# Attention feeding a channel-mix MLP: score banks held as three PSUM tiles of two banks, the last query tile of two head pairs as one group, the value product in the MLP's two banks

## The chip, the cores and the metric

The kernel runs on one core of one Trainium2 chip. The metric is device time in microseconds (us) of one execution. The engines that matter are TensorE (PE; its weight loads are listed as PEld), VectorE (DVE), ScalarE (ACT), GpSimd (POOL) and SyncE (SP, which here only issues DMAs). PSUM, where TensorE writes, has eight banks of 512 float32 per partition; a bank is what one matrix product is summed in. Each engine takes its instructions in the order in which they stand in its own queue.

## The reference, cut to what matters

All arrays are float32. Batch 8, 12 heads, sequence 448, head size 64; the MLP (called "MoE" in the code) has width 768 and inner width 1024.

```python
q_n, k_n = rmsnorm(q, g_q), rmsnorm(k, g_k)
scores = q_n @ k_n.T / sqrt(64)
attn = softmax(scores)
x = (attn @ v) laid out as [8, 448, 768]      # heads side by side
x_prev = x shifted by one position, zero first
xk = mu_k * x + (1 - mu_k) * x_prev
xr = mu_r * x + (1 - mu_r) * x_prev
out = sigmoid(xr @ w_r) * (relu(xk @ w_k) ** 2 @ w_v)
```

## The kernel before, in words

**Precision.** Every operand of a large product is split into a high and a low float16 half, and each product is three matmuls (high by high, high by low, low by high), summed in PSUM.

**Units of work.** Attention goes by head *pairs* (six per batch, 48 in all); two pairs form a *quad*, which shares the load and the normalisation of q and k (`prep`, L162 to L194: ACT squares, POOL and DVE sums, a reciprocal square root on DVE whose small operands lie in a PSUM bank called `misc`, and DMA transposes into the tiles `stk`). The 448 queries of a pair are seven tiles of 64. A *group* is two such tiles for both heads, 128 rows of scores per bank: `group_scores` (L240) issues six matmuls into two PSUM banks named `sc`, then for each bank a maximum on DVE (L260) and the exponential with its row sum on ACT (L261). The seventh tile of a pair is a group by itself, with one bank. `group_probs` (L265) takes the reciprocal of the sums (L273, L274), writes the high half of the probabilities on ACT (L279) and the low half on DVE (L280) into `ph`, and one DMA transpose (two for the seventh tile, L286) puts them into `pT`. After a pair's last group `attend` (L291) makes the value product, 22 matmuls into a bank named `av`, and ACT copies it out (L305).

**Scale of v.** `vprep` (L196) finds a power of two for each pair's v: a square with row sum on ACT, one small matmul into the `av` bank (L207), a maximum from there on DVE (L209), three small DVE operations, then the halves `vh` and `vl`.

**The MLP.** `moe(b)` (L450) runs behind attention. Its products are tiles named `mm`, in a ring of two banks: eight tiles of 18 matmuls for xk by w_k, then tiles of 18 (xr by w_r) and 24 (kk by w_v), all from line L460; ACT (L482, L516) or DVE (L519) reads a tile out. In the first part of the run the weights are converted as well (`weight_tile`, L394): they use the `mm` ring and, for their scales, the `av` bank.

**PSUM.** One bank `misc`, one `av`, four `sc`, two `mm`.

**What sets the order.** Three generators (attention, weights, MLP) are stepped in turn by a clock of their own: an attention step counts 1/126 of a batch (`ATT_STEPS`), an MLP step 1/93, and the MLP of batch b starts at b + 1.25. That gives the program order. A scheduler then places the instructions of each engine by its own timing model; those of the scores are preferred by 400 places (`QK_PRIORITY`). What program order fixes in any case is who gets a bank next: tiles of one name take the buffers of their ring in turn, so the third `mm` tile can start only when the first has been read out.

## Time and profile before

| | |
|---|---|
| median of three runs | 1214.28 us (1214.15 to 1221.72) |
| profiled execution, own time | 1216.88 us |
| its span, first to last instruction | 1215.1 us |
| mean granted TensorE clock | 0.934 |
| first value product read out | 91.0 us |
| 14th of 48 | 399.5 us |
| 48th of 48 | 1128.0 us |
| from there to the end (the MLP alone) | 87.1 us |

The run has three stretches. Up to some 300 us the weights are converted beside attention. From then to 1128 us attention and the MLP share TensorE. Then the MLP of the last batch runs alone. A row of the views by group reads: line, engine, operation, output tile from input tiles, shapes, count, then busy time and mean of one, then the idle time of the engine just before these instructions and what ended it.

### The profile page before, as it was taken

The page shows a single profiled execution, that of the slowest core. Times are in us where ns is not written, and L with a number is a line of the kernel's source. Part 1 is how long each engine was busy: PE and PEld are TensorE (multiplying, and loading weights), DVE is VectorE, ACT ScalarE, POOL GpSimd, SP SyncE. Part 2 cuts the span into 40 slices and gives each one's busy share as a digit, 9 for nine tenths or more (in the row PEclk, how much of TensorE's full clock was granted, in tenths as well). Part 3 has the DMA queues.
Part 4 walks back from the last instruction along what each step waited for, and adds up shares of the span by engine and source line. Part 5 has one row for each costly group of instructions (what it writes and reads, how often), then busy time and mean ns, then how long its engine had stood idle before and what let it go on. Part 6 is the DMA issues. An engine that isn't in the chain of part 4 may idle for free. (4 is left out here: it accounts for less than half of the span.)

```text
span 1215.1 us, 18885 instructions
## 1 busy us (share of the span) xinstructions
PE 996.6 (82%) x5935; PEld 476.4 (39%) x5935; DVE 828.9 (68%) x2357; ACT 794.8 (65%) x1756; POOL 672.3 (55%) x678
## 2 busy tenths in 40 slices
PE   1135545686788899999999999999899799999998
PEld 0012222243344344443444444444444354445464
DVE  4577788887977577676877676857775578666200
ACT  3366668677767767677778776777687477865411
POOL 2644357645558645585657564765586257523821
PEclk9996566888989999999999999999999899999999
DMA  7898889978789878878988897797897887885001
GB/s 160 147 182 169 162 165 218 191 152 151 143 139 161 152 123 162 150 129 158 162 154 154 155 170 141 134 167 146 143 157 129 128 148 135 137 158 90 13 14 39
DMA packets 456356, 172.77 MB, mean 142 GB/s; under 512 B 411200, under 2 KB 452672, under 8 KB 456256
## 3 DMA queue, kind: packets, MB, share of 16 engines
q1 hardware_dynamic: 423328, 132.24, 64.2%
q10 hardware_dynamic: 32928, 39.34, 13.8%
q8 instruction: 46, 0.75, 0.3%
q14 instruction: 54, 0.44, 0.1%
HBM read 61.41 MB, written 11.01 MB: 60 GB/s over the span
## 5 line engine op out<-in xcount | busy, mean ns | idle before, releaser
L261 ACT ACTIVATE sc<-sc,sums 128x448 f32<-128x448 f32 x336 | 201.6, 608 | 108.0 <-DVE sums L260 99.4
L280 DVE SCALAR_TENSOR_TENSOR ph<-sc,sums,ph 128x448 f16<-128x448 f32 x336 | 218.3, 677 | 68.4 <-ACT ph L279 66.1
L238 PE MATMUL sc<-stk 64*128 64x448 f16 (+1 forms) x1152 | 190.3, 380 | 68.3 <-DVE ph L280 45.9
L460 PE MATMUL mm<-wvh,kk 128*128 128x384 f16 x896 | 236.5, 332 | 4.0 <-DVE th L519 4.0
L460 PE MATMUL mm<-xk,wkh 128*128 128x448 f16 x768 | 217.8, 363 | 11.6 <-ACT kf L482 10.1
L260 DVE TENSOR_REDUCE sums<-sc 128x1 f32<-128x448 f32 x336 | 196.3, 613 | 37.3 <-PE sc L238 36.7
L279 ACT ACTIVATE ph<-sc,sums 128x448 f16<-128x448 f32 x336 | 195.2, 642 | 31.9 <-DMA pT<-ph 10.1
L238 PE MATMUL av<-pT,vh 128*64 128x448 f16 x672 | 145.8, 387 | 63.4 <-DMA pT<-ph 49.9
L460 PE MATMUL mm<-wrh,xr 128*128 128x384 f16 x672 | 177.1, 327 | 3.1 <-ACT xr L377 2.4
L460 PEld LDWEIGHTS <-kk 128*128 128x128 f16 x1344 | 126.5, 99 | 111.2 <-issue 36.6
L460 PE MATMUL mm<-wvl,kk 128*128 128x384 f16 x448 | 148.9, 332 | 0.0
L460 PE MATMUL mm<-xk,wkl 128*128 128x448 f16 x384 | 139.2, 363 | 0.0
L189 POOL TENSOR_TENSOR nat<-qk,nat 128x896 f16<-128x896 f32 x48 | 91.3, 1903 | 67.6 <-ACT nat L187 67.6
L238 PEld LDWEIGHTS <-stk 64*128 64x128 f16 (+1 forms) x1152 | 56.0, 100 | 184.1 <-issue 138.9
L170 POOL TENSOR_TENSOR xs<-xs 128x448 f32<-128x448 f32 x48 | 55.7, 1160 | 127.1 <-ACT xs L169 126.8
L460 PEld LDWEIGHTS <-xr 128*128 128x128 f16 x1008 | 93.6, 98 | 78.8 <-issue 16.2
L375 DVE SCALAR_TENSOR_TENSOR df<-x,bsc,df 128x448 f32<-128x448 f32 x90 | 90.3, 1014 | 32.7 <-POOL df L374 32.1
L273 DVE TENSOR_SCALAR sums<-sc 128x1 f32<-128x1 f32 x336 | 49.6, 151 | 89.9 <-ACT sc L261 88.5
L182 POOL TENSOR_TENSOR qk<-qk,ss 128x896 f32<-128x896 f32 x48 | 80.1, 1689 | 54.8 <-DVE ss L70 44.7
L460 PE MATMUL mm<-wrl,xr 128*128 128x384 f16 x336 | 109.7, 327 | 0.0
L460 PEld LDWEIGHTS <-wkh 128*128 128x128 f16 x768 | 73.9, 100 | 91.3 <-issue 35.5
L238 PEld LDWEIGHTS <-vh 128*64 128x64 f16 x672 | 59.5, 117 | 113.7 <-issue 67.3
(117 smaller groups left out, 1576.8 us busy)
## 6 DMA issues: line engine op xcount, KB each, us to landing
vf<-in_v_dram SPq DMA_DIRECT2D x48, 224.0 KB, 3.8
qk<-in_k_dram ACTq DMA_DIRECT2D x48, 224.0 KB, 4.8
qk<-in_q_dram ACTq DMA_DIRECT2D x48, 224.0 KB, 5.1
out_dram<-o SPq DMA_DIRECT2D x56, 192.0 KB, 2.9
vf<-in_v_dram SPq DMA_DIRECT2D x48, 192.0 KB, 3.8
raw<-in_moe_w_k_dram ACTq DMA_DIRECT2D x16, 384.0 KB, 4.4
raw<-in_moe_w_v_dram ACTq DMA_DIRECT2D x12, 512.0 KB, 4.4
raw<-in_moe_w_r_dram ACTq DMA_DIRECT2D x12, 384.0 KB, 4.7
```

The source lines that it names most:

```text
L170: nc.gpsimd.tensor_tensor(out=xs[:, :, 0:HD // 2], in0=xs[:, :, 0:HD // 2], in1=xs[:, :, HD // 2:], op=ALU.add)
L182: nc.gpsimd.tensor_tensor(out=tv, in0=tv, in1=spread(y[:, 2 * NT * n:2 * NT * (n + 1)], HD), op=ALU.mult)
L189: nc.gpsimd.tensor_tensor(out=lo, in0=t4, in1=hi, op=ALU.subtract)
L238: return op(**kw)
L260: nc.vector.tensor_reduce(out=sums[:, t:t + 1], in_=sp[:, 0:S], axis=AX.X, op=ALU.max, negate=True)
L261: nc.scalar.activation(out=sp[:, 0:S], in_=sp[:, 0:S], func=AF.Exp, bias=sums[:, t:t + 1], accum_out=sp[:, S:S + 1])
L273: nc.vector.tensor_scalar(out=r[:, j:j + 1], in0=sp[:, S:S + 1], scalar1=1e-9, scalar2=2.0 ** -15, op0=ALU.add, op1=ALU.mult)
L279: nc.scalar.activation(out=ph[:, j, 0:S], in_=sp[:, 0:S], func=AF.Copy, scale=r[:, j:j + 1])
L280: nc.vector.scalar_tensor_tensor(out=ph[:, j, S:], in0=sp[:, 0:S], scalar=r[:, j:j + 1], in1=ph[:, j, 0:S], op0=ALU.mult, op1=ALU.subtract)
L375: nc.vector.scalar_tensor_tensor(out=df, in0=xc, scalar=sc[:, MX + j:MX + j + 1], in1=df, op0=ALU.mult, op1=ALU.add)
L460: nc.tensor.matmul(out=ps_, lhsT=la(i, a), rhs=ra(i, c), start=(i == 0 and a + c == 0), stop=(i == n - 1 and a == 1))
```

## The change

The `misc` and `av` banks go. Two banks remain for the ring `mm`, and six go to scores, as three tiles of two banks.

- **Scores.** A group always fills one two-bank tile. `scores` takes one maximum over both banks in one DVE instruction, and `probs` one operation for both row sums. There are two exponentials and two copies per group as before.
- **Seventh tile.** The seventh query tiles of the two pairs of a quad form one group of twelve matmuls, placed fourth of seven groups. Four small transposes follow it, as two followed each of the two groups before. A quad has seven groups in place of eight.
- **Value product, scale of v, weight scales.** They take their bank from the ring `mm`, in turn with the MLP's tiles and the weights'. The small matmul for the scale of the next pair's v is written into the last 64 columns of the value product's bank, right behind the product, and ACT copies it to SBUF (a new instruction for each pair), where DVE takes the maximum. The square for it is issued at the end of the pair before, and `vprep` of a pair runs during that pair's own first groups. The load of the next pair's v is issued inside `vprep`.
- **prep.** The small operands of the reciprocal square root lie in SBUF.
- **Counts.** `ATT_STEPS` is 123; attention has 117 steps per batch, where it had 120 and `ATT_STEPS` was 126. The six xk tiles of a batch's last pair are mixed three and three, not in three twos.

The diff, cut to its core:

```diff
-ATT_STEPS = 126
+ATT_STEPS = 123
...
-    misc = ps.tile([P, 512], F32, name="misc", bufs=1)
-
     def allmax(src, n, r):
-        pt = ps.tile([P, 512], F32, name="av", bufs=1)
+        pt = ps.tile([P, 512], F32, name="mm", bufs=MM_BUFS)
...
-    rsqrt(nc, gm[:, 1:2], misc[:, 510:511], misc[:, 511:512])
+    rsqrt(nc, gm[:, 1:2], gm[:, 0:1], gm[:, 5:6])
...
-        o = (u % 2) * 2 * NSS
-        ss, tm = misc[:, o:o + NSS], misc[:, o + NSS:o + 2 * NSS]
+        sst = small.tile([P, 2 * NSS], F32, name="sst", bufs=2)
+        ss, tm = sst[:, 0:NSS], sst[:, NSS:]
...
+    def vsquare(i):
+        vf = VF[i]
+        vh = ap_.tile([P, 2, NT, HD], F16, name="vh", bufs=2)
+        vs = small.tile([P, 2 + HD], F32, name="vs", bufs=2)
+        nc.scalar.activation(out=vh[0:HD].rearrange("p h t d -> p h (t d)").bitcast(BF16), in_=vf[0:HD], func=AF.Square, accum_out=vs[0:HD, 0:1])
+        VS[i] = vh, vs
+
+    def vsum(i, dst):
+        vs = VS[i][1]
+        nc.tensor.matmul(out=dst, lhsT=vs[0:HD, 0:1].bitcast(BF16)[:, 1:2].broadcast_to([HD, P]), rhs=ident16[0:HD, 0:HD], start=True, stop=True)
+        nc.scalar.copy(out=vs[:, 2:], in_=dst)
...
         if hp == 0:
             BS[b] = small.tile([P, 2 * NP], F32, name="bstat", bufs=3)
         st = BS[b]
         vf = VF.pop(i)
-        vh = ap_.tile([P, 2, NT, HD], F16, name="vh", bufs=2)
+        vh, vs = VS.pop(i)
         vl = ap_.tile([P, 2, 4, HD], F16, name="vl", bufs=2)
-        vs = small.tile([P, 2], F32, name="vs", bufs=2)
-        pt = ps.tile([P, 512], F32, name="av", bufs=1)
-        nc.scalar.activation(out=vh[0:HD].rearrange("p h t d -> p h (t d)").bitcast(BF16), in_=vf[0:HD], func=AF.Square, accum_out=vs[0:HD, 0:1])
-        nc.tensor.matmul(out=pt[:, 0:HD], lhsT=vs[0:HD, 0:1].bitcast(BF16)[:, 1:2].broadcast_to([HD, P]), rhs=ident16[0:HD, 0:HD], start=True, stop=True)
-        yield
-        nc.vector.tensor_reduce(out=vs[:, 1:2], in_=pt[:, 0:HD], axis=AX.X, op=ALU.max)
         sv, iv = st[:, hp:hp + 1], st[:, NP + hp:NP + hp + 1]
+        nc.vector.tensor_reduce(out=vs[:, 1:2], in_=vs[:, 2:], axis=AX.X, op=ALU.max)
...
+        if i + 1 < len(pairs):
+            vload(i + 1)
         yield
...
-    def group_scores(i, t0, n):
-        T = TQ[i]
-        if t0 == 0:
-            SUMS[i] = small.tile([P, 32], F32, name="sums")
-        sums = SUMS[i]
-        banks = []
-        for j in range(n):
-            banks.append(ps.tile([P, 512], F32, name="sc", bufs=4))
+    def scores(g):
+        u, x, t0 = g
+        both = ps.tile([P, 2, 512], F32, name="sc", bufs=3)
+        sums = small.tile([P, 4], F32, name="sums", bufs=6)
...
             for m, (kl, ql) in enumerate(((0, 0), (0, 1), (1, 0))):
-                for h in (1, 0):
-                    hs = slice(h * HD, (h + 1) * HD)
-                    last = after(last, nc.tensor.matmul,
-                        out=banks[h][:, 0:S] if n == 2 else banks[0][hs, 0:S],
-                        lhsT=T[hs, 1, ql * NT + t0:ql * NT + t0 + n].rearrange("p t c -> p (t c)"),
-                        rhs=T[hs, 0, kl * NT:(kl + 1) * NT].rearrange("p t c -> p (t c)"),
-                        start=(m == 0), stop=(m == 2))
-        for j, sp in enumerate(banks):
-            t = t0 + j
-            nc.vector.tensor_reduce(out=sums[:, t:t + 1], in_=sp[:, 0:S], axis=AX.X, op=ALU.max, negate=True)
-            nc.scalar.activation(out=sp[:, 0:S], in_=sp[:, 0:S], func=AF.Exp, bias=sums[:, t:t + 1], accum_out=sp[:, S:S + 1])
-            SC[i, t] = sp
-            yield
-
-    def group_probs(i, t0, n):
-        sums = SUMS[i]
-        if t0 == 0:
-            PT[i] = ap_.tile([P, 2, NT, S], F16, name="pT", bufs=PT_BUFS)
-        pT = PT[i]
-        r = sums[:, 16 + t0:16 + t0 + n]
-        sps = [SC.pop((i, t0 + j)) for j in range(n)]
-        for j, sp in enumerate(sps):
-            nc.vector.tensor_scalar(out=r[:, j:j + 1], in0=sp[:, S:S + 1], scalar1=1e-9, scalar2=2.0 ** -15, op0=ALU.add, op1=ALU.mult)
+                for i in (2 * u + x,) if t0 < NT - 1 else (2 * u, 2 * u + 1):
+                    T = TQ[i]
+                    for h in range(2):
+                        hs = slice(h * HD, (h + 1) * HD)
+                        if t0 < NT - 1:
+                            dst, n = both[:, h, 0:S], 2
+                        else:
+                            o = (h + i % 2) % 2 * HD
+                            dst, n = both[o:o + HD, i % 2, 0:S], 1
+                        last = after(last, nc.tensor.matmul, out=dst,
+                            lhsT=T[hs, 1, ql * NT + t0:ql * NT + t0 + n].rearrange("p t c -> p (t c)"),
+                            rhs=T[hs, 0, kl * NT:(kl + 1) * NT].rearrange("p t c -> p (t c)"),
+                            start=(m == 0), stop=(m == 2))
+        nc.vector.tensor_reduce(out=sums[:, 0:2], in_=both[:, :, 0:S], axis=AX.X, op=ALU.max, negate=True)
+        SC[g] = both, sums
+        for j in range(2):
+            nc.scalar.activation(out=both[:, j, 0:S], in_=both[:, j, 0:S], func=AF.Exp, bias=sums[:, j:j + 1], accum_out=both[:, j, S:S + 1])
+            yield
+
+    def probs(g, gi):
...
+        for i in (2 * u + x,) if t0 < NT - 1 else (2 * u, 2 * u + 1):
+            if i not in PT:
+                PT[i] = ap_.tile([P, 2, NT, S], F16, name="pT", bufs=PT_BUFS)
+        r = sums[:, 2:4]
+        nc.vector.tensor_scalar(out=r, in0=both[:, :, S], scalar1=1e-9, scalar2=2.0 ** -15, op0=ALU.add, op1=ALU.mult)
...
-        for j in range(n):
-            sp = sps[j]
...
+        for j in range(2):
+            nc.scalar.activation(out=ph[:, j, 0:S], in_=both[:, j, 0:S], func=AF.Copy, scale=r[:, j:j + 1])
+            nc.vector.scalar_tensor_tensor(out=ph[:, j, S:], in0=both[:, j, 0:S], scalar=r[:, j:j + 1], in1=ph[:, j, 0:S], op0=ALU.mult, op1=ALU.subtract)
+        if t0 < NT - 1:
             nc.sync.dma_start_transpose(
-                out=pT.rearrange("p a c r -> p (a c) r")[:, :, t0 * HD:(t0 + n) * HD], in_=ph.rearrange("p a c -> p (a c)"))
+                out=PT[2 * u + x].rearrange("p a c r -> p (a c) r")[:, :, t0 * HD:(t0 + 2) * HD], in_=ph.rearrange("p a c -> p (a c)"))
...
+            for y in range(2):
+                for h in range(2):
+                    o = (h + y) % 2 * HD
+                    nc.sync.dma_start_transpose(out=PT[2 * u + y][:, h, :, t0 * HD:], in_=ph[o:o + HD, y, :])
+        yield
...
-        av = ps.tile([P, 512], F32, name="av", bufs=1)
+        av = ps.tile([P, 512], F32, name="mm", bufs=MM_BUFS)
...
+        if i + 1 < len(pairs):
+            with tc.issue_after(last.ins):
+                vsum(i + 1, av[:, S:])
...
+        NQ = len(quads)
+        groups = [(u, *g) for u in range(NQ) for g in ((0, 0), (0, 2), (0, 4), (0, NT - 1), (1, 0), (1, 2), (1, 4))]
...
+        vsquare(0)
+        av = ps.tile([P, 512], F32, name="mm", bufs=MM_BUFS)
+        vsum(0, av[:, S:])
+        yield
         yield from vprep(0)
...
+        pre = vp = iter(())
+        yield from scores(groups[0])
+        for gi, g in enumerate(groups):
+            u, x, t0 = g
+            i = 2 * u + x
+            if x == 0 and t0 == 0 and u + 1 < NQ:
+                pre = prep(u + 1)
+            if gi and t0 == 0:
+                vp = vprep(i)
...
+            next(vp, None)
+            yield
+            done = (t0 == NT - 1) if x == 0 else (t0 == NT - 3)
+            if done:
+                for h in (vp,) + ((pre,) if x else ()):
+                    for _ in h:
                         yield
-                if i + 2 < N:
-                    vload(i + 2)
+                if i + 1 < len(pairs):
+                    vsquare(i + 1)
                 if x and u + 2 < NQ:
                     load(u + 2)
             if gi + 1 < len(groups):
-                yield from group_scores(*groups[gi + 1])
-            yield from group_probs(i, t0, n)
-            if t0 == 6:
+                yield from scores(groups[gi + 1])
+            yield from probs(g, gi)
+            if done:
                 yield from attend(i)
             b, hp = pairs[i]
-            if hp == NP - 1 and t0 >= 2:
...
-        for d in {2: (0, 1), 4: (2, 3), 6: (4, 5)}[t0]:
+        for d in {2: (0, 1, 2), 4: (3, 4, 5)}[t0]:
...
-        pg = ps.tile([P, 512], F32, name="av", bufs=1)
+        pg = ps.tile([P, 512], F32, name="mm", bufs=MM_BUFS)
```

What this does to the order on TensorE is seen at two places. The rows give line, operation, output tile from its inputs with buffer numbers, and the output's size; `xr` and `kk` are the MLP's inputs, `wr` and `wv` its weights, `pT` the transposed probabilities, `vh` and `vl` the halves of v, `stk` the transposed q and k.

First, before the change, at the value product of the 29th pair:

```order
L460 MATMUL mm_7670<-wrh_109,xr_5206 128x384
L460 LDWEIGHTS xr_5206
L460 MATMUL mm_7670<-wrl_110,xr_5206 128x384
L238 LDWEIGHTS vh_6843
L238 MATMUL av_7233<-pT_7045,vh_6843 64x448
L460 LDWEIGHTS xr_5206
L460 MATMUL mm_7670<-wrh_109,xr_5206 128x384
L460 LDWEIGHTS xr_5206
L460 MATMUL mm_7670<-wrh_109,xr_5206 128x384
```

One matmul of the value product stands alone between matmuls of the MLP; seven MLP matmuls follow it, then the other 21. The changed kernel, at the value product of the same pair:

```order
L244 MATMUL mm_6983<-pT_6804,vh_6688 64x448
L244 LDWEIGHTS vl_6776
L244 MATMUL mm_6983<-pT_6804,vl_6776 64x448
L244 LDWEIGHTS stk_6928
L244 MATMUL sc_7192<-stk_6928 128x448
L244 LDWEIGHTS stk_6928
L244 MATMUL sc_7192<-stk_6928 128x448
```

Here the value product is cut by scores, which come in whole groups of six, and no MLP matmul stands inside it. Over the whole program the sequence of large and small matmuls changes its kind (scores, value product, MLP, weights, scale of v) 684 times before and 423 times now: 685 and 424 stretches. Up to the 14th value product it is 155 and 127 of them. Up to the 14th value product the MLP has had 444 of its 3504 matmuls before and 414 now; up to the 48th and last 3034 and 2718, so that 470 and 786 are left behind it. Between a pair's last score and its value product stand, over pairs 15 to 48, 58.5 MLP matmuls in the median (41 at least) before, and 115.5 (67 at least) now.

Second, the ring of two banks, in the changed kernel, at the end of the value product of the 30th pair:

```order
L244 MATMUL mm_7223<-pT_6966,vh_6946 64x448
L202 LDWEIGHTS vs_7184
L202 MATMUL mm_7223<-ident16_75,vs_7184 128x64
L474 LDWEIGHTS kk_5095
L474 MATMUL mm_7176<-wvh_109,kk_5095 128x384
...
L474 MATMUL mm_7176<-wvh_109,kk_5095 128x384
L474 LDWEIGHTS xr_5020
L474 MATMUL mm_7273<-wrh_107,xr_5020 128x384
```

Behind the value product in tile 7223 come the scale of v and the last six matmuls of tile 7176, and then at once the first matmul of tile 7273, which has the bank of 7176: it must wait until DVE has read 7176 out. Among the 38 places where a value product stands between two MLP tiles in the ring, 9 have no matmul at all between the earlier tile's last matmul and the next use of its bank. Before the change no tile of the MLP follows so closely.

43 lines of the change are left out of this document (12 added, 31 removed).

## The prediction

> **What bounds the kernel now.** I read the page's shares and slices first, then stretches chosen from them, then what TensorE does and waits for in the longest stretch. The page:
>
> ```profile
> PE 996.6 (82%) x5935; PEld 476.4 (39%) x5935; DVE 828.9 (68%) x2357; ACT 794.8 (65%) x1756; POOL 672.3 (55%) x678
> PE   1135545686788899999999999999899799999998
> DMA  7898889978789878878988897797897887885001
> ```
>
> No engine is full over the whole span, but TensorE is from about the thirteenth slice on. The same by stretch (length, then busy time of PE, PEld, DVE, ACT and POOL, the granted clock, the share of the DMA engines, GB/s):
>
> ```profile
> 60.00:243.00 183.00, 93.23 (x467) 42.02 (x465) 147.12 (x449) 122.27 (x255) 97.66 (x86) 0.71 0.90 181
> 560.00:702.00 142.00, 135.48 (x830) 63.34 (x827) 107.56 (x308) 107.54 (x245) 88.44 (x92) 0.99 0.87 153
> 400.00:1128.00 728.00, 683.07 (x4162) 320.81 (x4161) 515.14 (x1430) 516.54 (x1178) 419.26 (x435) 0.98 0.83 145
> 1128.00:1215.00 87.00, 80.48 (x470) 45.78 (x468) 12.07 (x15) 21.06 (x48) 35.15 (x39) 0.98 0.08 19
> ```
>
> From 400 to 1128 us TensorE is 94% busy, DVE and ACT 71%, the DMA engines 83%. The stretch begins at the 14th value product and ends at the 48th, as the ACT copies that follow them show (count, then first and last start; the first row is for the time up to 400.2 us):
>
> ```profile
> L305 ACT ACTIVATE x<-av,bstat x14: 614/634/672, 91.0 to 399.5; 128x448 f32<-128x448 f32 x14
> ...
> L305 ACT ACTIVATE x<-av,bstat x48: 614/637/732, 91.0 to 1128.0; 128x448 f32<-128x448 f32 x48
> ```
>
> So 34 pairs take 728 us, 21.4 us each. What fills TensorE there, by group (busy time is modelled and overlaps; I use counts and idle times):
>
> ```profile
> L238 PE MATMUL sc<-stk 64*128 64x448 f16 (+1 forms) x798 | 125.0, 357 | 14.5 <-DVE ph L280 12.9 <-DVE bstat L211 0.9 <-DVE bstat L213 0.7
> L238 PE MATMUL av<-pT,vh 128*64 128x448 f16 x476 | 98.2, 364 | 25.8 <-DMA pT<-ph 24.4 <-issue 0.9 <-DVE sums L260 0.4
> L238 PE MATMUL av<-pT,vl 128*64 128x448 f16 x272 | 61.9, 366 | 0.0
> L207 PE MATMUL av<-ident,vs 64*128 64x64 bf16 x33 | 6.6, 199 | 0.0
> ```
>
> The rest of the 4162 matmuls, 2583, is the MLP's. What one costs in a stream stands in the chain that ended last:
>
> ```profile
> 1071.88 1.49 PE sc L238 x12
> ...
> 1124.20 0.31 PE av L238
> 1124.50 1.24 PE mm L460 x6
> 1125.74 2.21 PE av L238 x21
> ...
> 1147.66 54.76 PE mm L460 x330
> ```
>
> A score matmul costs 1.49/12 = 0.124 us, one of the value product 2.21/21 = 0.105. The MLP's of 384 columns cost 54.76/330 = 0.166; the mean of both widths is 80.48/470 = 0.171 from the last stretch above. Then 2583 x 0.171 + 798 x 0.124 + 748 x 0.105 + 33 x 0.199 = 626 us of the 728. Attention's waits are 14.5 + 25.8 = 40 us. That leaves 62 us, and the order has 684 - 155 = 529 changes of kind in this stretch: **0.12 us per change**. The rows bound it from above: the lone value matmul costs 0.31 in place of 0.105, and the six behind it 1.24 in place of 6 x 0.166, together 0.45 for two changes, 0.22 each.
>
> So TensorE sets the pace here, and little of it is waiting: work 86%, changes of kind 8.5%, waits 5.5%.
>
> **The change part by part.**
>
> *Fewer changes of kind.* From the 14th value product on, 296 in place of 529, so 233 x 0.12 = 28 us less (51 us at 0.22; nothing, if the 62 us have another cause). Before it 28 fewer, 3 us.
>
> *MLP work moved behind attention.* The MLP is tied to program order, since its tiles and the value products take the two banks in turn. At the 14th value product it is 30 matmuls behind where it stood, at the 48th 316. So 286 x 0.171 = 49 us leave the stretch, 30 x 0.171 = 5 us the time before it, and 54 us are added to the end. Sum zero, if attention does speed up.
>
> *Waits for banks and transposes.* Three two-bank tiles hold three groups where four banks held two, so the 12.9 us for L280 should go. Between a pair's last score and its value product the order now has 115.5 MLP matmuls in the median and had 58.5; at 0.171 that is 20 us of cover and was 10. The chain that this must cover is, beside TensorE, a maximum, two exponentials, two copies and a transpose:
>
> ```profile
> L260 DVE TENSOR_REDUCE sums<-sc 128x1 f32<-128x448 f32 x336 | 196.3, 613 | 37.3 <-PE sc L238 36.7
> L261 ACT ACTIVATE sc<-sc,sums 128x448 f32<-128x448 f32 x336 | 201.6, 608 | 108.0 <-DVE sums L260 99.4
> L280 DVE SCALAR_TENSOR_TENSOR ph<-sc,sums,ph 128x448 f16<-128x448 f32 x336 | 218.3, 677 | 68.4 <-ACT ph L279 66.1
> L273 DVE TENSOR_SCALAR sums<-sc 128x1 f32<-128x1 f32 x336 | 49.6, 151 | 89.9 <-ACT sc L261 88.5
> L422 DVE TENSOR_REDUCE WSC<-av 128x1 f32<-128x128 f32 x20 | 5.7, 284 | 3.2 <-PE av L421 3.2
> pT<-ph SPq DMA_TRANSPOSE x240, 4.3
> ```
>
> Twice 0.613, 0.608 and 0.677, the last twice for the copy on ACT too, and 4.3 make about 10 us without queueing: today's cover is about the chain's length, the new one twice that. I take 30 of the 37 us (12.9 + 24.4) as gone, between none and all. Before the 14th pair the same waits are larger:
>
> ```profile
> PE sc L238 <- DVE ph L280: 33.0, 19, 6.0
> ```
>
> There the DMA engines are 90% busy and would be waited for next. I take 10 us, between 0 and 33.
>
> *A shared ring.* A new wait: an MLP tile that finds its bank still being read. The order has nine places with nothing in between. Behind such a tile on TensorE stand the next pair's scores and value product. The same wait exists now, when an MLP tile is late to be read out:
>
> ```profile
> PE mm L460 <- ACT kf L482: 10.1, 7, 5.3
> PE mm L460 <- DVE th L519: 4.0, 4, 2.3
> ```
>
> That is 1.4 and 1.0 us a time. For nine places and a few looser ones, 11 x 1.4 = 16 us; at least 0, at most all 38 places, 38 x 1.4 = 53. The Trainium skill, "Perfetto Trace Analysis", section Optimizing Tensor Performance, says that independent matmul groups should rotate through different banks, so that reading one out overlaps the next. By that rule this edit loses, and at the nine places it does; by the rows above the loss stays in the tens of us.
>
> *DVE and ACT.* A maximum over both banks, from 284 ns at 128 elements and 613 at 448, is (613 - 284)/320 = 1.03 ns per element, so about 1.07 us for 896: 168 of them save 168 x (2 x 0.613 - 1.07) = 26 us of DVE. 168 fewer L273 save 25 us, 24 fewer reciprocals 4. ACT gets 48 copies of 64 columns; the nearest copies out of PSUM are
>
> ```profile
> L516 ACT ACTIVATE th<-mm,bsc 128x128 f32<-128x128 f32 x144 | 42.7, 375 | 43.9 <-PE mm L460 42.7 <-POOL df L374 1.2
> L68 DVE TENSOR_TENSOR misc<-misc,gm 128x1 f32<-128x1 f32 x3 | 0.5, 155 | 0.0
> L117 DVE TENSOR_TENSOR gm<-gm 128x1 f32<-128x1 f32 x1 | 0.2, 152 | 0.0
> ```
>
> so at most 48 x 0.375 = 18 us. The last two rows, of one element each in PSUM and in SBUF, price the moved operands at 3 ns; I take nothing, with 360 such operations x 0.19 (L68's 28 columns) = 68 us of DVE as an end that would need each to double. With both engines at 71% all of this is off the path: TensorE is the cover. Were it gone, DVE's saving and ACT's loss would show at -55 and +18. Also hidden: the same 240 transposes in another order on SP, with v's load moved past a few of them, whose data is used a pair later.
>
> *What is late next: the DMA engines.* They are busy 0.83 x 728 = 604 us for these 34 pairs, and no transfer goes away. TensorE's terms alone would give 728 - 28 - 49 - 30 + 16 = 637 us, 18.7 per pair, and the DMA engines 95%. The longest stretch above with a high share holds 0.90 over 183 us; so I take 604/0.90 = **671 us**, 19.7 per pair. At 0.95 TensorE's 637 would decide.
>
> *The sum.* The 14th value product at 399.5 - 5 - 3 - 10 = 381.5 us; the 48th at 381.5 + 671 = 1052.5; the end 87 + 54 = 141 later: a span of 1193.5, where it was 1215.1. The profiled execution took 1.8 us more than its span and 2.6 us more than the median of the runs (1216.88, 1214.28), so **1193 us**.
>
> **The rivals.**
>
> *Attention does not speed up (slower).* The MLP used to fill every wait of attention: it is 316 matmuls further at its end than program order now allows. Tied to the value products it can't, and if DMA or the ping-pong of ACT and DVE holds attention at its pace, TensorE idles and the 54 us come at the end. With the DMA share at its present 0.83: 381.5 + 728 + 141 = 1250.5. The price of the place is fixed; the point from which it decides is 1215 - 141 - 381.5 = 692.5 us for the 34 pairs, 20.4 each, a DMA share of 0.87. For it: 0.87 is all that the stretch 560 to 702 reaches, DVE and ACT wait for each other (L261 99.4, L273 88.5, L280 66.1 us), and SP issues transposes in order. Against: the doubled cover, and 28 us of changes of kind that go whatever else happens. Chance 0.22.
>
> *The fused maximum is on the chain (slower).* The first exponential of a group waits 1.07 in place of 0.61 us. If each of the 3.5 x 34 = 119 groups passed that on, 55 us: 1248. For it: L261 waits for the maximum more than for anything. Against: ACT idles 29% of the stretch, so a delay of one group is taken up there while two others are in flight. The Trainium skill, "Perfetto Trace Analysis", section Optimizing Scalar/DVE Operations, has the rule that where such engines are not saturated but cause bubbles elsewhere, breaking instructions up may help; this edit does the reverse. No row here shows a fused maximum. Chance 0.04.
>
> *Even.* Between 20.0 and 20.8 us per pair, 1202 to 1226, which is 1% either way of the median, about what a measurement of this kernel can tell from no change: gain and tail cancel. Chance 0.16.
>
> *DMA allows more.* At 0.95 or above TensorE's own sum stands, 637 us: 1159; with a change of kind at 0.18, halfway to its bound, 14 us less, near DMA's 0.97: 1145. Chance 0.18.
>
> That the edit doesn't do what it says is excluded by the order of the rows.
>
> **How the numbers follow.** My forecast, 1165 to 1202, has 0.40, and with 0.18 for the lower case faster has 0.58; even 0.16; slower 0.26. The range, 1150 to 1245, leaves out the lowest cases (0.06) and the upper part of the two slower ones (0.12).
>
> **What would show it.** Right: value products end near 1050 us with some 140 us of MLP alone behind; DMA share near 0.90 in between; waits of scores for L280 nearly gone; MLP matmuls waiting for ACT or DVE some 15 us more; DVE 55 us less busy. Wrong: the last value product after 1074 us, TensorE waiting there for transposes or for a bank read late by ACT, or a DMA share still near 0.83.

## The result and the profile after

The changed kernel takes 1341.14 us in the median against 1214.22: a ratio of 1.104, with a 95% interval of 1.094 to 1.115. The prediction was 1193. The profiled execution took 1343.59 us, its span is 1341.8 us (1215.1 before), and the granted TensorE clock 0.885 (0.934).

The page of the changed kernel, shares and slices:

```profile
PE 969.6 (72%) x5935; PEld 483.7 (36%) x5935; DVE 848.8 (63%) x1996; ACT 810.2 (60%) x1804; POOL 667.8 (50%) x678
PE   0234343375779778897787788698787878999998
DMA  6679977784579797888796988877878867740001
```

TensorE no longer stands at nine tenths through the middle. Its value products end where the next rows say (count, first and last start; first row for the time up to 460 us), which is the reading on which everything below rests:

```profile
L315 ACT ACTIVATE x<-mm,bstat x14: 636/643/701, 95.3 to 459.3; 128x448 f32<-128x448 f32 x14
...
L315 ACT ACTIVATE x<-mm,bstat x48: 634/650/716, 95.3 to 1201.1; 128x448 f32<-128x448 f32 x48
```

So the 127 us between the spans are lost in three places:

| | before | predicted | measured | measured less before |
|---|---|---|---|---|
| 14th value product, us | 399.5 | 381.5 | 459.3 | +59.8 |
| the 34 pairs after it | 728.5 | 671 | 741.8 | +13.3 |
| behind the 48th | 87.1 | 141 | 140.7 | +53.6 |

The 13.3 us of the middle are about what a mere reordering does there (13.0 us in e16 below). What the middle lacks is the gain of 57 us that was to pay for the longer end.

The stretches (length, busy time of PE, PEld, DVE, ACT, POOL, the clock, the DMA share, GB/s):

```profile
459.00:1201.00 742.00, 609.01 (x3836) 299.80 (x3836) 499.88 (x1163) 509.62 (x1169) 394.09 (x413) 0.94 0.80 138
...
1201.00:1342.00 141.00, 133.31 (x788) 76.79 (x786) 17.71 (x24) 32.39 (x77) 54.40 (x61) 0.99 0.08 20
```

In the middle TensorE is 82% busy where it was 94%, and yet a pair takes 21.8 us where it took 21.4. DVE and ACT fell to 67% and 69%, the DMA engines to 80%: nothing took TensorE's place as the full engine. What TensorE waits for there, by group:

```profile
L474 PE MATMUL mm<-wvh,kk 128*128 128x384 f16 x576 | 151.9, 333 | 10.3 <-DVE th L533 5.2 <-ACT x L315 4.3 <-ACT th L530 0.6
L474 PE MATMUL mm<-xk,wkh 128*128 128x448 f16 x517 | 149.6, 371 | 26.1 <-ACT kf L496 15.8 <-ACT x L315 9.8 <-DVE th L533 0.4
L474 PE MATMUL mm<-wrh,xr 128*128 128x384 f16 x432 | 120.9, 348 | 30.1 <-ACT x L315 11.0 <-ACT th L530 9.5 <-DVE th L533 9.2
L244 PE MATMUL sc<-stk 64*128 64x448 f16 (+1 forms) x768 | 87.7, 372 | 55.5 <-DVE ph L285 39.5 <-DMA stk<-nat 15.7
L244 PE MATMUL mm<-pT,vh 128*64 128x448 f16 x476 | 83.3, 376 | 7.4 <-DVE th L533 6.2 <-ACT kf L496 1.0
```

The MLP's matmuls wait 10.3 + 26.1 + 30.1 = 66.5 us, nearly all of it for a bank that is still being read, and the value products 7 more. Before the change that was 5:

```profile
L460 PE MATMUL mm<-wvh,kk 128*128 128x384 f16 x672 | 177.2, 331 | 1.7 <-DVE th L519 1.7
L460 PE MATMUL mm<-xk,wkh 128*128 128x448 f16 x546 | 152.2, 357 | 2.2 <-ACT kf L482 2.2
L460 PE MATMUL mm<-wrh,xr 128*128 128x384 f16 x504 | 133.1, 327 | 0.7 <-ACT th L516 0.7
```

Value products wait no longer for transposes (24.4 us before). But scores wait longer for a score bank, 39.5 us for L285 where it was 12.9, although three tiles hold more, and 15.7 us for the transposed q and k, for which they did not wait before.

ACT, which the prediction called covered, waits in the same stretch, after the change and before it:

```profile
ACT ph L284 <- DMA pT<-ph: 37.6, 28, 2.9
ACT vh L197 <- DMA vf<-in_v_dram: 36.7, 28, 3.0
ACT sc L269 <- DVE sums L266: 31.4, 36, 2.2
```

```profile
L279 ACT ACTIVATE ph<-sc,sums 128x448 f16<-128x448 f32 x234 | 136.2, 645 | 17.9 <-ACT sc L261 7.2 <-DMA pT<-ph 5.1 <-issue 3.5
L206 ACT ACTIVATE vh<-vf 64x896 bf16<-64x896 f32 x33 | 31.3, 948 | 1.7 <-DMA vf<-in_v_dram 1.7
ACT sc L261 <- DVE sums L260: 77.4, 54, 4.8
```

The first wait, 5.1 us before, is for one of the two probability buffers to be emptied by its transpose. The second, 1.7 us before, is of the square of the next pair's v, for a load that is now issued inside the same pair. All that is queued behind them on ACT, exponentials included, waits too. The third, for the maximum, has fallen from 77.4 us.

### The profile page after: what moved, and what is told of

Read it like the earlier page. It is cut to its first block, busy times and chain, and to the rows that moved or that the text cites. A ratio compares the mean times of both kernels' runs of the same rounds, so it can differ in the third digit from the quotient of the medians.

```text
span 1341.8 us, 18540 instructions
## 1 busy us (share of the span) xinstructions
PE 969.6 (72%) x5935; PEld 483.7 (36%) x5935; DVE 848.8 (63%) x1996; ACT 810.2 (60%) x1804; POOL 667.8 (50%) x678
## 5 line engine op out<-in xcount | busy, mean ns | idle before, releaser
L285 DVE SCALAR_TENSOR_TENSOR ph<-sc,sums,ph 128x448 f16<-128x448 f32 x336 | 225.6, 678 | 154.4 <-ACT ph L284 153.1
L284 ACT ACTIVATE ph<-sc,sums 128x448 f16<-128x448 f32 x336 | 210.1, 637 | 107.3 <-DMA pT<-ph 56.5
L474 PE MATMUL mm<-xk,wkh 128*128 128x448 f16 x768 | 227.1, 379 | 43.5 <-ACT kf L496 15.8
L244 PE MATMUL sc<-stk 64*128 64x448 f16 (+1 forms) x1152 | 145.5, 404 | 136.0 <-DVE ph L285 103.1
L474 PE MATMUL mm<-wvh,kk 128*128 128x384 f16 x896 | 234.0, 331 | 12.2 <-DVE th L533 7.1
L474 PE MATMUL mm<-wrh,xr 128*128 128x384 f16 x672 | 186.1, 344 | 43.5 <-ACT x L315 19.5
L266 DVE TENSOR_REDUCE sums<-sc 128x2 f32<-128x896 f32 x168 | 180.8, 1080 | 16.6 <-PE sc L244 16.6
L474 PEld LDWEIGHTS <-kk 128*128 128x128 f16 x1344 | 129.9, 99 | 110.9 <-issue 31.8
L474 PE MATMUL mm<-wvl,kk 128*128 128x384 f16 x448 | 148.1, 331 | 0.0
L474 PEld LDWEIGHTS <-xr 128*128 128x128 f16 x1008 | 101.2, 102 | 126.8 <-issue 64.7
L474 PE MATMUL mm<-xk,wkl 128*128 128x448 f16 x384 | 144.7, 377 | 0.0
L244 PE MATMUL mm<-pT,vh 128*64 128x448 f16 x672 | 123.4, 391 | 25.7 <-DMA pT<-ph 8.4
L474 PEld LDWEIGHTS <-wkh 128*128 128x128 f16 x768 | 78.1, 104 | 128.5 <-issue 73.5
L244 PEld LDWEIGHTS <-stk 64*128 64x128 f16 (+1 forms) x1152 | 47.5, 104 | 210.5 <-issue 154.7
L474 PE MATMUL mm<-wrl,xr 128*128 128x384 f16 x336 | 116.0, 345 | 0.0
L498 POOL TENSOR_TENSOR kf<-kf 128x448 f32<-128x448 f32 x64 | 60.0, 938 | 97.5 <-ACT kk L497 95.3
L389 DVE SCALAR_TENSOR_TENSOR df<-x,bsc,df 128x448 f32<-128x448 f32 x90 | 82.9, 928 | 34.2 <-POOL df L388 34.2
L534 POOL TENSOR_TENSOR o<-th,bsc 128x384 f32<-128x384 f32 x48 | 41.1, 857 | 104.7 <-DVE th L533 69.8
```

The lines of the kernel that those rows point to most:

```text
L244: return op(**kw)
L266: nc.vector.tensor_reduce(out=sums[:, 0:2], in_=both[:, :, 0:S], axis=AX.X, op=ALU.max, negate=True)
L284: nc.scalar.activation(out=ph[:, j, 0:S], in_=both[:, j, 0:S], func=AF.Copy, scale=r[:, j:j + 1])
L285: nc.vector.scalar_tensor_tensor(out=ph[:, j, S:], in0=both[:, j, 0:S], scalar=r[:, j:j + 1], in1=ph[:, j, 0:S], op0=ALU.mult, op1=ALU.sub ...
L389: nc.vector.scalar_tensor_tensor(out=df, in0=xc, scalar=sc[:, MX + j:MX + j + 1], in1=df, op0=ALU.mult, op1=ALU.add)
L474: nc.tensor.matmul(out=ps_, lhsT=la(i, a), rhs=ra(i, c), start=(i == 0 and a + c == 0), stop=(i == n - 1 and a == 1))
```

## The experiments

Each run is read by the same three numbers: the 14th value product, the 34 pairs after it, and what lies behind the 48th. "MLP left" is the number of MLP matmuls behind the last value product in the run's order. Where the MLP's matmuls are left out the output is not the reference's; these three runs (e5, e6, e11) and e7 are one execution each.

| run | median us | 14th at | 34 pairs | behind | MLP left |
|---|---|---|---|---|---|
| before | 1214 | 399.5 | 728.5 | 87.1 | 470 |
| changed | 1341 | 459.3 | 741.8 | 140.7 | 786 |
| e1 before, shared ring of two | 1312 | 423.4 | 749.3 | 137.3 | 768 |
| e2 before, shared ring of three | 1281 | 398.9 | 746.3 | 132.8 | 754 |
| e3 changed, own bank, two score tiles | 1397 | 460.4 | 846.2 | 87.7 | 450 |
| e4 changed, ATT_STEPS 114 | 1284 | 442.4 | 747.7 | 88.7 | 480 |
| e5 changed, no MLP matmuls | 1226 | 432.5 | 720.3 | 70.0 | |
| e6 before, no MLP matmuls | 1144 | 398.7 | 714.3 | 29.3 | |
| e7 changed, weights' scales in score ring | 1314 | 427.5 | 744.1 | 140.7 | 786 |
| e8 before, five score banks | 1300 | 418.5 | 742.9 | 138.4 | 774 |
| e9 changed, two maxima | 1328 | 447.2 | 737.3 | 140.7 | 786 |
| e10 changed, e4 and e7 together | 1289 | 430.8 | 765.1 | 88.8 | 480 |
| e11 changed, no MLP, third ph buffer | 1196 | 417.3 | 705.9 | 70.6 | |
| e12 before, second value bank | 1236 | 411.6 | 735.3 | 87.2 | 471 |
| e13 before, prep in SBUF | 1247 | 418.2 | 736.3 | 87.0 | 473 |
| e14 before, third ph buffer | 1246 | 411.1 | 735.1 | 96.1 | 532 |
| e15 the same, ATT_STEPS 122 | 1218 | 414.0 | 715.1 | 87.1 | 471 |
| e16 before, ATT_STEPS 122 | 1232 | 402.3 | 741.5 | 87.1 | 465 |
| e17 before, prep in SBUF, 122 | 1234 | 410.8 | 735.6 | 87.1 | 470 |
| e18 before, prep in SBUF, 124 | 1245 | 417.5 | 734.8 | 92.2 | 507 |

**Is it the shared ring or the two-bank groups?** First the ring alone, in the kernel before:

```diff
-        av = ps.tile([P, 512], F32, name="av", bufs=1)
+        av = ps.tile([P, 512], F32, name="mm", bufs=MM_BUFS)
...   # the same for the scale of v (L205), the weights' scales (L414) and L92
```

> The kernel before, with one edit: its value products, its scale of v and the weights' scales take their bank from the MLP's ring of two, in place of a bank of their own; scores stay in four single banks, one bank lies idle. Theory R (the shared ring costs the time): at least 80 us over before, 1290 to 1340; the 14th value product after 430 us, where it was 399.5 before and 459.3 in the changed kernel; some 768 MLP matmuls behind the last one, as in its order, worth 50 us. Theory G (the two-bank score groups cost it): 1215 to 1270, no more than the longer end, with the 14th value product near 400 us.

1311.67 us, a ratio of 1.082 (1.069 to 1.095), as theory R had it but for the 14th value product, which came at 423 and not after 430. The ring alone, with scores untouched, brings 97 of the 127 us by the medians; in the profiled execution these are 24 up to the 14th, 21 in the 34 pairs and 50 behind.

With `MM_BUFS = 3` besides:

> As the run before it in this call, with three banks in the shared ring (all eight are then in use). Theory R: a third bank takes away most waits for a bank, so the 14th value product is back near 400 us; the order still leaves 754 MLP matmuls behind the last one, so 1215 to 1265. Theory G: the same time as with two banks, within 1.5%.

1281.43 us: a third bank takes the loss out of the first part (398.9) and leaves the rest. That is 16 us above theory R's range and 2.3% below the time with two banks, where theory G had it within 1.5%; the 34 pairs stay 18 us longer.

Then the groups without the ring, in the changed kernel:

```diff
-        both = ps.tile([P, 2, 512], F32, name="sc", bufs=3)
+        both = ps.tile([P, 2, 512], F32, name="sc", bufs=2)
-        av = ps.tile([P, 512], F32, name="mm", bufs=MM_BUFS)
+        av = ps.tile([P, 512], F32, name="av", bufs=1)
...   # av likewise in allmax, weight_tile and the first vsum
```

> The changed kernel, with a bank of its own again for value products, scale of v and weights' scales; scores have two tiles of two banks in place of three. The rest of the change stays: one maximum for both banks, both banks freed together, the joined last tiles. Theory R: most of the loss is gone, 1200 to 1250, the 14th value product before 415 us. Theory G: the two-bank groups cost it, and more so with two tiles: at least 1300.

1397.26 us, the slowest of all, so theory G is right of this kernel: the end is short again (87.7), but a pair takes 24.9 us. On four banks, two tiles that are each freed as a whole do worse than four single banks in the kernel before (21.4 us), though e3 differs from that kernel in the rest of the change too. Against the changed kernel it differs in the banks alone: having the third tile in place of a bank of their own for the others is worth 104 us in the 34 pairs, and it is what leaves only two banks for all the rest. Both theories hold, each for its half of the trade.

**The first part.** The tile for the weights' scales leaves the ring:

```diff
-        pg = ps.tile([P, 512], F32, name="mm", bufs=MM_BUFS)
+        pg = ps.tile([P, 2, 512], F32, name="sc", bufs=3)[:, 0, :]
```

> The changed kernel, with the tile for the weights' scales (20 of them, in the first 300 us) taken from the ring of score tiles and not from the MLP's ring of two. Theory R: the first stretch loses its 60 us there, since converting a weight tile, its scale and a value product take turns in two banks; the 14th value product comes back from 459 to 400 to 430 us, the whole to 1285 to 1315. Theory G (the two-bank groups hold the first stretch too): 14th after 445, no gain, since the score ring is used more.

1314.46 us, with the 14th value product at 427.5, as theory R had it: 32 of the 60 us, and nothing changes elsewhere. In the changed kernel these are the two longest of TensorE's waits between 60 and 459 us; the second names it (L430 is the scale's matmul, L424 the last step of converting a weight tile, which holds a bank of the ring; in e7 the second is 13.0 us):

```profile
PE sc L244 <- DVE ph L285: 63.6, 21, 11.1
PE mm L430 <- DVE wf L424: 40.5, 10, 14.3
```

**The end.** Only the interleaving is shifted:

```diff
-ATT_STEPS = 123
+ATT_STEPS = 114
```

> The changed kernel with ATT_STEPS 114 in place of 123, which hands the MLP more steps per attention step: 480 MLP matmuls are left behind the last value product in place of 786, the rest stands within attention. Theory T (the longer end is a loss by itself, since TensorE has idle time earlier): 52 us less than the changed kernel, 1280 to 1300. Theory R: the MLP's tiles in the ring then hold the value products up as much as they shorten the end: 1325 to 1350.

1283.91 us, 57 less, as theory T had it. The end is 88.7 us, and the 34 pairs, which by the order now hold 2556 MLP matmuls in place of 2304 (43 us of TensorE at 0.171), take 747.7 in place of 741.8:

```profile
442.00:1190.00 748.00, 641.42 (x4112) 322.78 (x4112) 502.35 (x1176) 525.57 (x1199) 411.37 (x432) 0.96 0.78 140
```

TensorE had the room, which speaks against TensorE as what sets the pace. The chain of work that ended last can be followed back through all 34 pairs in this run; its shares of that time by line, the twelve largest (issue is time without a wait that the profile shows):

```profile
by line: DMA pT<-ph 12.5%; PE mm L474 10.4%; issue 8.6%; DMA qk<-in_q_dram 6.1%; DMA stk<-nat 5.9%; DVE sums L266 4.9%; DVE ph L285 4.5%; ACT sc L269 4.4%; ACT ph L284 4.0%; DMA vf<-in_v_dram 3.6%; DMA qk<-in_k_dram 3.1%; ACT xs L166 1.8%;
```

Summed by engine over all lines, transfers have 31% of it, DVE and ACT 17% each, and TensorE 13%, most of it the MLP's matmuls (L474). So with TensorE 86% busy, at a granted clock of 0.96 and with the whole MLP, its work is a small part of the path. Both repairs at once:

> The changed kernel with two of its three losses undone at once: ATT_STEPS 114, and the tile for the weights' scales in the score ring. If they are separate, the gains add: 1341 - 57 - 27 = 1257, with the 14th value product near 430 us, 745 us for the 34 pairs and 89 us behind. If one hides the other, no less than 1280. Neither theory has it below the kernel before.

1288.86 us, no better than e4 alone. The first part and the end are as expected (430.8, 88.8), but the 34 pairs take 765 us, 21 us more than in e7. By e4 the same step from 123 to 114 cost 6 us; here it is half of the 43 that it would cost if TensorE set the pace, so the count of matmuls alone does not settle it. TensorE is as busy there as in e4 (645 and 642 us) and scores wait longer for L285 (56.6 us, 34.2 in e4). The gains don't add, and why this order is slower in the middle is open.

**What sets attention's pace.** One matmul of 18 or 24 is left of each MLP product, in the changed kernel and in the one before (in short):

```diff
                 for a, c in ((0, 0), (0, 1), (1, 0)):
-                    nc.tensor.matmul(out=ps_, lhsT=la(i, a), rhs=ra(i, c), ...)
+                    # only (i, a, c) = (0, 0, 0) is issued
```

> The changed kernel with one matmul in place of 18 or 24 in each MLP product, so 176 of them in place of 3504; everything that ACT, DVE, GpSimd and the DMA engines do stays, and the output is not the reference's. Read by the time of the 34 pairs between the 14th and the 48th value product, 742 us in the changed kernel. Theory P (TensorE sets attention's pace, as predicted): below 670 us, 19.7 per pair or less, where the DMA engines would take over. Theory C (attention is held by its own chain of transposes, loads and the in-order queues of ACT and DVE, and the MLP's matmuls only fill): above 700.

> The kernel before with the same matmuls taken away (176 in place of 3504, the output is not the reference's). Read by the same 34 pairs, 728 us before. Theory P: below 670. Theory C: above 700.

The 34 pairs take 720.3 and 714.3 us: 95% of the MLP's matmuls gone, and a pair is 2 to 3% faster. That is theory C, in both kernels. The kernel before without them, over its 34 pairs, and what TensorE waits for there:

```profile
398.00:1113.00 715.00, 358.50 (x1712) 133.94 (x1708) 513.47 (x1429) 512.90 (x1169) 421.05 (x436) 0.64 0.83 147
```

```profile
PE sc L238 <- DVE ph L280: 158.4, 56, 8.4
PE av L238 <- DMA pT<-ph: 124.6, 51, 9.8
```

The waits that looked like 40 us beside the MLP are 283 us without it. Beside the MLP its matmuls stood in them. One reservation: with TensorE half idle its granted clock is 0.63 to 0.64 in these pairs, and attention's own matmuls are slower: in e6 a score matmul has 462 ns in the mean where it had 357, one of the value product (vh) 535 where it had 364. At full clock the pairs might go faster, by how much no run shows. The chain of e4 carries no such reservation, and neither does the next run.

More score banks alone, in the kernel before:

```diff
-            banks.append(ps.tile([P, 512], F32, name="sc", bufs=4))
+            banks.append(ps.tile([P, 512], F32, name="sc", bufs=5))
...   # prep's operands in SBUF, which frees the fifth bank
```

> The kernel before with the operands of prep in SBUF, as in the change, and the bank that this frees given to scores: five single banks in place of four; nothing is shared. Its order has 774 MLP matmuls behind the last value product, as the changed kernel has 786. Theory P: scores wait less, TensorE sets the pace, the 34 pairs take 670 to 690 us with the fewer MLP matmuls and the total is 1195 to 1220. Theory C: the 34 pairs stay at 715 to 740 and the longer end comes on top: 1255 to 1275.

1299.51 us. As theory C had it, but worse than its range: the 34 pairs take 743 us, no less, the end 138 us, and the first part is 19 us longer. Its stretch from the 14th to the 48th value product:

```profile
418.50:1161.40 742.90, 649.59 (x3831) 292.44 (x3830) 519.60 (x1399) 496.55 (x1130) 395.31 (x412) 0.95 0.78 138
```

In e13 below, which has all of this but the fifth bank, the 34 pairs hold 2537 MLP matmuls by the trace and take 736.3 us; here they hold 2274. TensorE has some 45 us less to do (263 at 0.171, an estimate), its clock is 0.95, and no pair is faster. That is theory P's case without any sharing, and it fails. Here nothing is shared, and still 774 MLP matmuls are left behind. So the longer end is not the ring's doing alone: in this order too the MLP's matmuls stand later against attention.

A third buffer for the probabilities, in the changed kernel without MLP matmuls, by `PH_BUFS = 3` and an inner MLP tile cut to seven row blocks:

> As the changed kernel without the MLP's matmuls (176 of 3504 stay), with a third buffer for the probabilities ahead of their transposes; the inner MLP tile is one row block smaller to make room; the output is not the reference's. Read by the 34 pairs, 720 us without the third buffer. If ACT's wait for the transposes to leave these buffers (46 us in that run) holds the pace, 675 to 700. If it only moves the wait to the next stage (the two pT tiles, or the loads), 710 to 730.

The 34 pairs take 705.9 us, between the two cases: ACT's wait for these buffers falls from 48 us to 2, and 14 us came through. That is one execution, and about as much as reordering alone moves these pairs.

**The fused maximum.** Two instructions, one for each bank:

```diff
-        nc.vector.tensor_reduce(out=sums[:, 0:2], in_=both[:, :, 0:S], axis=AX.X, op=ALU.max, negate=True)
+        nc.vector.tensor_reduce(out=sums[:, 0:1], in_=both[:, 0, 0:S], axis=AX.X, op=ALU.max, negate=True)
+        nc.vector.tensor_reduce(out=sums[:, 1:2], in_=both[:, 1, 0:S], axis=AX.X, op=ALU.max, negate=True)
```

> The changed kernel with the maximum over the two banks split into two instructions, one for each bank; all else stays. If the fused maximum delays the chain, as the prediction's second slow case has it, the 34 pairs between the 14th and 48th value product take less than in the changed kernel (742 us), by up to 55, and the total falls below 1325. If it only saves DVE time off the path, the total is 1335 to 1355.

1327.96 us, between the two ranges: 4.5 us in the 34 pairs and 12 before them. If this is the fused instruction it is a tenth of the 55 us priced for it; it is also within what a mere reordering does, as follows.

**Single edits of the kernel before, and how much the order alone does.** The freed bank as a second one for value products; prep's operands in SBUF alone; and the third probability buffer, with the MLP's `kf` moved to make room, at two interleavings:

```diff
-        ss, tm = misc[:, o:o + NSS], misc[:, o + NSS:o + 2 * NSS]
+        sst = small.tile([P, 2 * NSS], F32, name="sst", bufs=2)     # e12, e13, e17, e18
-    av = ps.tile([P, 512], F32, name="av", bufs=1)
+    av = ps.tile([P, 512], F32, name="av", bufs=2)                  # e12
-PH_BUFS = 2
+PH_BUFS = 3                                                         # e14, e15
-ATT_STEPS = 126
+ATT_STEPS = 122                                                     # e15, e16, e17; 124 in e18
```

> The kernel before with the operands of prep in SBUF, and the bank that this frees given to the value products as a second one; nothing is shared, scores keep four single banks. Its order leaves 471 MLP matmuls behind the last value product, as before (470). If the first stretch is held by weights' scales, scale of v and value products in one bank, the 14th value product comes before 390 us and the total is 1190 to 1208. If attention's own chain holds it, 1208 to 1225.

> The kernel before with one edit: prep's small operands lie in SBUF, as in the change; the freed bank stays empty. Theory S (these operations take two to four times longer beside GpSimd and sit in prep's serial chain): the loss of the run with the second value bank returns, 1225 to 1245, with the 14th value product 8 to 15 us later than before. Theory P0 (they cost nothing, as the prediction's sum had it): 1208 to 1222.

> The kernel before with a third buffer for the probabilities; to make room the MLP's kf tiles lie in another pool (in the first batch they share a ring with the mixing). Its order leaves 532 MLP matmuls behind the last value product in place of 470, worth 10 us. If these buffers hold attention's pace, the 34 pairs fall to 700 to 715 us and the total to 1190 to 1210. If not, 1215 to 1235.

> As the run before it in this call, with ATT_STEPS 122 in place of 126, whose order leaves 471 MLP matmuls behind the last value product, as in the kernel before. If the buffers hold the pace: 1180 to 1200. If not: 1208 to 1230.

> The kernel before with ATT_STEPS 122 in place of 126, which only shifts how attention and the MLP are interleaved; its order leaves 465 MLP matmuls behind the last value product (470 before). If order alone matters little: 1205 to 1225. If order alone scatters the time by 2%, as two of the runs suggest: outside that, in either direction.

> The kernel before with prep's operands in SBUF and ATT_STEPS 122; 470 MLP matmuls are left behind the last value product. If the SBUF operands cost 20 to 30 us by themselves, it is slower than the run before it in this call by that much. If the loss at ATT_STEPS 126 came from the order that the edit happened to bring, the two are within 10 us.

> The kernel before with prep's operands in SBUF and ATT_STEPS 124; 507 MLP matmuls left, worth 6 us over 470. A third order of the same edit: at least 1230 if the SBUF operands cost 20 to 30 us, 1210 to 1228 if it was the order.

e12 is 1.021 (1.015 to 1.027) of before, e13 1.026 (1.023 to 1.029), e14 1.026 (1.022 to 1.030), e15 1.003 (1.000 to 1.005). Taken alone, e13 would say that prep in SBUF costs 33 us. But e16, where one number shifts the interleaving and nothing else changes, is 1.014 (1.010 to 1.019), outside the range for an order that matters little, and e17, the SBUF edit at that same shift, is only 2.8 us above it. e18, a third order of the SBUF edit, is 1.026 (1.022 to 1.030) of before and lies where its expectation had a cost of the operands by themselves. So the two tests of that cost disagree: it is between 3 and 33 us and stays open. The order by itself moves this kernel by some 17 us, 126 is the better of the two orders tried without another edit, and single edits of 30 us or less can't be priced by one pair of totals. e12 and e14 came above both of their cases, and e13 just above its slower one. What repeats better is the first part: with prep in SBUF the 14th value product comes at 410.8 to 418.2 in all four runs that change little else (e12, e13, e17, e18), without it at 399.5 and 402.3. That would be 8 to 19 us of the changed kernel's 60. It is not the only thing that moves this part: e14 and e15, which keep prep in PSUM and move the MLP's `kf`, come at 411.1 and 414.0. The third buffer likewise: e15 is 13.6 us faster than e16 at the same interleaving, e14 32 us slower than the kernel before at 126, with 9 us of that in the end. e15 came where its second case had it, the buffers not holding the pace, though its 715.1 us are the shortest 34 pairs of all runs with the whole MLP. None of the versions that compute the whole result beats the kernel before.

## Why the prediction was wrong, point by point

**The step that failed** is "So TensorE sets the pace here, and little of it is waiting". TensorE was 94% busy because the MLP's matmuls, which wait for little, were put wherever attention left a gap. Its waits beside them, 40 us, measured the gaps that were left over, not those that attention makes: 283 us, by e6 at its lower clock. Attention's pair takes 21.0 us without the MLP's matmuls, 21.4 with them, and 21.8 after the change (21.2 without them). The 28, 49 and 30 us that were subtracted for TensorE did not shorten the 34 pairs: TensorE had less to do and waited instead, and the pairs took 742 us where 671 were forecast. The pace is set, as the chain of e4 shows, by transfers, DVE and ACT in turn, with TensorE at 13%. Followed back by the same rule from each value product to the one before, TensorE has 108 of the 485 us that can be followed in the kernel before, and 75 of 728 in the changed one.

*Changes of kind.* The price about holds: in the changed kernel's 34 pairs the same sum, by the trace 2287 MLP matmuls, 768 of scores, 748 of value products and 33 small ones, gives 571 us of work; 133 us are idle in the groups above and the scale of v (4.0), and 742 - 571 - 133 = 38 us are left for 296 changes, 0.13 us each, or less, since single matmuls were up to 6% slower too (xr 348 ns, 327 before). Where 62 us were left before, it is 38 now: TensorE did save some 24 us; it spent them waiting.

*MLP work moved behind attention.* 54 us predicted, 53.6 measured. "Sum zero, if attention does speed up" was the condition, and it failed. The term was right and its cover was gone.

*Waits for banks and transposes.* TensorE's waits for transposes went from 24.4 us to none, as the doubled cover said, but ACT's wait for the same transposes rose from 5.1 to 37.6. Waits for a score bank rose, from 12.9 to 39.5; that scores no longer have the MLP in front of them is the likely reason and not shown. Of 37 us, 30 were taken as gone; 39.5 us stand there now.

*The shared ring.* 16 us taken, 53 the bound; about 74 us of waits in the 34 pairs alone, 5 before. The count of nine places was right as a count of the tightest ones. It left out that the value product's own bank is read out by ACT, whose queue is now held by the waits shown above: 25 us of the 74 are for L315. And it was priced in the middle only. In the first part, where weights take turns in the same two banks, it is 24 us by e1, and taking one user out gives 32 by e7. There the prediction subtracted 18 us and the run added 60.

*DVE and ACT.* DVE did the fused maximum as worked out, and ACT's copy cost less than its bound. But DVE is not 55 us less busy: 849 us where it had 829. The moved operands did not cost 3 ns:

```profile
L266 DVE TENSOR_REDUCE sums<-sc 128x2 f32<-128x896 f32 x168 | 180.8, 1080 | 16.6 <-PE sc L244 16.6
...
L68 DVE TENSOR_TENSOR sst<-sst,ss 128x28 f32<-128x28 f32 x72 | 24.0, 333 | 1.0
...
L172 DVE TENSOR_SCALAR sst<-sst 128x14 f32<-128x14 f32 x24 | 17.6, 733 | 0.2
...
L203 ACT COPY vs<-mm 128x64 f32<-128x64 f32 x48 | 10.6, 221 | 5.1 <-PE mm L202 2.6 <-DVE mm L423 1.5 <-DVE ss L70 0.7
```

L68 and L172, on prep's operands, take 189 and 172 ns in PSUM. The rows that I took, of one element, run at the start, where GpSimd has nothing else to do. Over the run these operations take 143 us in place of 92: 51 of the 68 us at the far end of that bound, and a row that is alike in size but not in company was the wrong one to be near to. The load of v, called hidden, was not: 36.7 us of ACT's waits where it had 1.7.

*DMA as the next limit* was never reached: the share is 0.80.

**The rivals.** "Attention does not speed up" was the right one, with a chance of 0.22, and its mechanism is what happened: 728 us for the pairs and 141 behind were priced, 742 and 141 came. Its sum of 1250.5 missed by 91 us, 78 of them in the first part, which stood in it at 381.5 and came at 459.3. No variant with the MLP in it came under the point from which it decides, 20.4 us per pair; the best, e15, had 21.0. The fused maximum as a rival is not borne out at its price: e9 gives 4.5 us, and ACT's wait for the maximum fell from 77.4 to 31.4. In the even case 20.8 us per pair make 1229 and not 1226. The range ended at 1245, below even that rival's own sum, and no case let the first part get slower: I had bounded its gain from both sides, and its loss not at all, though two of the edits (the ring for weights, prep in SBUF) lie there.

**What stays open.** Of the 60 us before the 14th value product, 24 to 32 are the ring's and 8 to 19 may go with prep's operands; the rest, and how these overlap, is not settled. What holds a pair at 21 us is not one resource: with the MLP gone DVE and ACT are busy 72% and the DMA engines 83%. That it is the chain through transfers and the in-order queues of DVE and ACT is what the chain of e4 shows, as far as its releasers go, which are inferred from semaphores; which link to shorten is open, and no run here shortens one by more than reordering does.

## What to carry to other kernels

An engine that is full because low-priority work is put into its gaps looks like the bound and isn't: take that work away, or look at what the other stream's pace does where its density changes, or follow the chain back and see how much of it that engine has, before subtracting anything from that engine. Banks that two streams share in program order tie the one to the other, so work that used to fill gaps can be left over for the end; count in the new order what is left behind the last step, and ask what happens to that count if the speed-up doesn't come. When a scheduler places everything, first measure how far a mere reordering moves the time, here 1.4%, and read smaller effects by stage and not by total.

## What the runs showed of the hardware that was not expected

Small DVE operations on SBUF that run beside a GpSimd instruction are mostly held up until it ends. In the mean the 28-element ones take 0.298 to 0.333 us where they had 0.189 in PSUM, the 14-element ones with a scalar 0.733 to 0.831 against 0.172 (e13 and the changed kernel against the kernel before). The run that has prep in SBUF alone shows the same:

```profile
L172 DVE TENSOR_SCALAR sst<-sst 128x14 f32<-128x14 f32 x24 | 19.9, 831 | 0.0
```

These means mix two kinds. In the changed kernel, beside a GpSimd instruction that ends at 647.21 us, and without one (start, duration):

```profile
645.14 2.07 POOL L169 TENSOR_TENSOR qk<-qk,gq 128x896 f32<-128x896 f32 x1
645.86 1.38 DVE L172 TENSOR_SCALAR sst<-sst 128x14 f32<-128x14 f32 x1
...
694.99 0.16 DVE L172 TENSOR_SCALAR sst<-sst 128x14 f32<-128x14 f32 x1
```

Of L68's 72 operations in the changed kernel, 52 have no GpSimd instruction beside them and take 0.160 to 0.190 us; the 20 that have one take 0.727 us in the mean, 15 of them over 0.25. On PSUM, in the kernel before, 30 beside one and 42 without both take 0.189. In the changed kernel 78 operations on prep's operands took over 0.25 us (L173, usually 0.29, over 0.4), and every one of them ended 0.03 to 0.07 us after the end of a GpSimd instruction; in e13 it is 63 of 63.

The Trainium skill, "SBUF — State Buffer", section Who interferes with whom, says that DVE and GpSimd share a pair of SBUF ports as an exclusive lock, that a DVE instruction with two SBUF inputs contends with a GpSimd instruction that reads SBUF (the 28-element rows have two), and that `tensor_scalar` can, when its operands meet certain conditions, enter a mode that uses the shared pair as well (the 14-element rows). The rows above agree with it; which mode the 14-element rows ran in no trace here shows.
